# An MLP whose second stage uses eight block products in the last two visits of the first pair, and begins later in the second visit

## The chip, the cores and the metric

The kernel runs on one core of one Trainium2 chip. The metric is the device time of one execution in microseconds (us); every figure without a unit is in us. The profile comes from one execution and names the engines PE (TensorE, the matmuls), PEld (its weight loads), DVE (VectorE), ACT (ScalarE), POOL (GpSimd) and SP (SyncE, whose queue issues the DMAs).

## The reference

A transformer block on 2048 tokens of width D = 576: attention with 32 heads of 18 and one shared key and value head, then an MLP with F = 4608. The change lies in the MLP, whose core is:

```
y = layernorm(x)
h = gelu(y @ w1 + b1)        # (2048 x 576) @ (576 x 4608), tanh form
out = h @ w2 + b2            # (2048 x 4608) @ (4608 x 576)
x = x + gb * out
```

All is float32. A scale `gb` and the shift and scale ahead of `y` come from a small product of the condition vector; they are folded into the weights and into the normalised rows before the MLP starts.

## The kernel before

**Stages.** Attention takes the first 1400 us or so; while it runs, GpSimd prepares the MLP's weights and stores them in DRAM (`w1scr`, `w2scr`, `w2sum`). Then comes the MLP, a loop over 36 *visits* (`for v in range(NV)`, `NV = 2 * NG`, `NG = 18`). The tokens are taken in two *pairs* of two blocks of 512; the visits 0 to 17 serve the first pair, 18 to 35 the second. One visit does 256 of the 4608 hidden features for one pair: both stages are therefore 2 by 2 block problems (two blocks of tokens, two halves of the features or of the width).

**Precision.** A float32 number is split into a high part, rounded to the matmul's type (FP32R), and a low part, the rest. A product is three matmuls: high by high, high by low, low by high. Making a high part is a cast or a copy, making a low part a subtraction. `ops` (28 slots) and `opt` hold the parts of the first stage's inputs, `GT` (the buffers `big`, `gt` and a piece of `w1a`) those of its outputs, addressed by *unit* number.

**First stage, with seven products.** By Strassen's method, in Winograd's form, the four blocks of the first stage come from seven block products A11, S2, S3, A12, S1, A22, S4 (`product`, L1053 of the kernel before), in that order in each visit. Six matmuls of 128x512 make one; four of them take two more with the operands of width 64 that are left over (`opt`, the *tails* t0 and t1). VectorE adds the results up (`u`, L1250, L1257, L1273, L1282, L1291), and `gelu` (L1062 to L1074) runs in three steps on ScalarE and VectorE. A gelu result `h` is copied to a unit's high part by ScalarE (L1071), and GpSimd makes its low part (L1074). `psB` has four buffers in PSUM.

**Second stage, with seven products.** `sums(v)` forms four sums of the four gelu blocks on GpSimd: four additions or subtractions (L1126 to L1135), four casts (L1123) and four low parts (L1124). `fc2s(v)` then does seven *pieces*, in the order of `SEVEN`. A piece is 12 matmuls of 128x288 into two `psA` tiles of 128x576 (L1150) and two VectorE additions from them (L1156), into the output rows `XT` or into `eb`. There are two `psA` buffers. After its last use, each piece's weights are loaded anew for the next visit (`load_w2s`, one DMA of 288 KB). The very last visit (35) has no sums: `fc2` does the four blocks as eight plain block products, 96 matmuls of 128x288 in eight pieces, one `psA` tile and one addition (L1184) per 128 tokens.

**What sets the order.** The order is written by hand: each engine does its instructions in the order in which the code issues them. Between two products the loop calls `t_()` (the next piece of the second stage), `s_()` (the next sum), `g_()` (the next step of every running gelu) and `more()` (forming operands, or layernorm and output work). `fc2s(v)` is appended at the end of visit v, so its pieces run in visit v + 1; a visit has seven `t_()`, the first between A11 and S2, and the last piece of a visit's seven runs as the first of the visit after the next. Visit 1 has only six: its first piece comes between S2 and S3.

**Forming the operands of the second pair.** `op_pieces` cuts the 14 operands out of `yr`. For the second pair this is done in visits 17 and 18, each operand as soon as its slot has been used for the last time. In the code "+X" is the high part of X by ScalarE (L974), "-X" the low part (L976), "=X" a difference of two slices of `yr` (L967). The table `at` gives each operand's slot, its slice of `yr` and the engine of its low part: `ve` is VectorE, `e2` is GpSimd for the second pair. Ahead of visit 17 stand the last transposes (L152) of the layernorm, whose results ScalarE copies to `yr` (L162); the layernorm's rows lie in two buffers named `Z2`.

**DMAs.** All go through SP's queue in the order of issue. An issue that waits for a buffer holds those behind it. First-stage weights (`w1a`, eight DMAs per visit) are reloaded right after the product that used them.

Of the kernel before, what the change touches and what calls it, by code (L numbers as in the profile page):

```python
# [8 lines left out]
F32 = mybir.dt.float32  # L9
# [23 lines left out]
def block_kernel(ctx: ExitStack, tc, x, wqkv, wo, w1, b1, w2, b2, c, wmod, ident_in, out):  # L33
# [922 lines left out]
    def op_pieces(R, e2):  # L956


        at = {"B11": (0, 0, ve), "B21": (2, 2, e2), "B22": (4, 7, e2), "T2": (6, 5, ve), "T1": (8, 5, ve),
              "T3": (10, 0, ve), "T4": (12, 2, e2), "t0": (0, 4, e2), "t1": (1, 9, e2)}  # L960
        less = {"T3": (5, 0, 0), "T4": (2, 5, 2), "T1": (7, 5, 5)}
# [57 lines left out]
    EB = [px.tile([128, 4, 288], F32, name="eb"), BC[:, :2, :].rearrange("p r (h c) -> p (r h) c", c=288)]  # L1019
    W2, W2S, GT = [], [], []  # L1020

    def wo_end():
# [4 lines left out]
        a.append(W1["r"][:, 31:40].rearrange("p a b -> p (a b)").rearrange("p (f c) -> p f c", f=2))  # L1027
        W2.extend(a[:2])
        W2S.extend(t.rearrange("p f (n c) -> p (f n) c", c=288)[:, i:i + 2] for t in a for i in (0, 2))
# [6 lines left out]
    NV = 2 * NG  # L1036

    def load_w2(v):
        for l in range(2):
            sy.dma_start(W2[l].bitcast(F32), w2scr[v % NG, :, l])  # L1040

# [14 lines left out]
    def gelu(v, f, b, p):  # L1056

        u = GU["A%d%d" % (2 - b, 2 - f)][v % 2] if v == NV - 1 or (b, f) != (0, 1) else None
        h = HB[:, 2 * b + f, :]
# [25 lines left out]
    GU["A21"] = GU["S3"]  # L1085
    GU["A22"] = 6, 7

    def xb(v, b, nn, j):
# [49 lines left out]
    def fc2s(v):  # L1138

        bank = []  # L1140
        for k, (w, first, to) in enumerate(SEVEN):
            gh, gl = (unit(GU[w][v % 2], l) for l in range(2))
            for j in range(2):
# [11 lines left out]
                else:  # L1155
                    ve.tensor_tensor(o, p[:, :, :288], o, op=ALU.add)  # L1156
            if v + 2 < NV:
                load_w2s((v + 1) % NG, k)
            else:
                if k == 3:  # L1160
                    load_w2(v + 1)
                if k > 3:
                    eb_add(v, *((1, 0), (1, 1), (0, 1))[k - 4])
# [3 lines left out]
    def fc2(v):  # L1167
        h2, l2 = W2
        for bt in range(2 * NT):
            b, t = divmod(bt, NT)  # L1170
            p = psA()
            ts_ = slice(128 * t, 128 * (t + 1))
            for nn in range(2):
                cs = slice(288 * nn, 288 * (nn + 1))
                terms = []
                for f in range(2):
                    gh, gl = (unit(GU["A%d%d" % (2 - b, 2 - f)][1], l)[:, ts_] for l in range(2))
                    terms += [(gh, h2[:, f, cs]), (gh, l2[:, f, cs]), (gl, h2[:, f, cs])]
                for q, (x, y) in enumerate(terms):
                    pe.matmul(p[:, nn, :288], x, y, start=(q == 0), stop=(q == len(terms) - 1))  # L1180
            tt = 2 * NT + bt
            X = XT[:, tt, :]
            Xv = X.rearrange("p (a b) -> p a b", a=2)
            ve.tensor_tensor(Xv, p[:, :, :288], Xv, op=ALU.add)  # L1184
            sy.dma_start(out[128 * tt:128 * (tt + 1), :], X)
            yield
# [21 lines left out]
    for v in range(NV):  # L1208
# [35 lines left out]
        more("+B11", "+T4")  # L1244
        if v > 1:
            t_()
# [3 lines left out]
        ve.tensor_tensor(U[:, 0], bb, U[:, 0], op=ALU.add)  # L1250
        t_()
        g_()
# [6 lines left out]
        more("-T2 =T3", "+B22", True)  # L1259
        t_()  # L1260
        product(ba, "A12", 2, False, (0, 0))
# [15 lines left out]
        more("-T3 -B21")  # L1277
        t_()
        g_()
        product(bc, "A22", 12, False, (1, 0))  # L1280
# [5 lines left out]
        more("=T4 +t0")  # L1286
        t_()
        g_()
        product(bd, "S4", 4, False, (2, 1))
# [60 lines left out]
```

## Time and profile before

| | before |
|---|---|
| time, median of 3 runs | 2281.99 (2280.32 to 2283.00) |
| the profiled execution: its time, its span | 2280.29, 2278.5 |
| mean granted TensorE clock | 0.996 |
| MLP, first matmul of visit 1 to the end of the span | 1425.64 to 2278.5 |
| an undisturbed visit (19) | 22.84 |
| GB/s over the span | 129 (read 200.48 MB, written 93.19 MB) |
| 128x512 subtraction on POOL (L1124), x140 | 1299 ns |
| 128x512 gelu step on DVE (L1065), x144 | 684 ns |
| 128x512 ScalarE activation (L1062), x144 | 680 ns |

How to read it: busy shares are averages over stages with different limits. A row of a timeline has the start, the duration, the engine, the line, the operation, the output and inputs by name, their shapes, and in brackets the idle time of that engine just before, with the instruction that ended it. In the table of waits the columns are the waiting engine and line, what it waited for, the sum, the number of times and the longest. A stretch of the table of stretches shows the busy time of each engine with the number of instructions, then the granted TensorE clock, the DMA share and GB/s. The durations of matmuls that follow each other overlap, so their rate is read from start to start.

### The profile page before, as it was taken

The numbers are of one execution on the slowest core, as the hardware profiler recorded it, in microseconds if no ns is written. First come the engines' busy times: TensorE is split into PE (matmuls) and PEld (weight loads), VectorE is DVE, ScalarE is ACT, GpSimd is POOL, SyncE is SP. The second block draws the span as 40 slices with busy tenths as digits, with TensorE's granted clock in tenths as the row PEclk, the third lists the DMA queues.
The fourth block names the chain that finished last, engine by engine and source line by source line (L and its number), as shares of the span: only waits on it lengthen the run. The fifth ranks groups of instructions, "written<-read, shape, count | busy, mean of one in ns | idle before, by whom it ended". The sixth has DMA issues, their size and how long they took to land.

```text
span 2278.5 us, 45948 instructions
## 1 busy us (share of the span) xinstructions
PE 2241.0 (98%) x16534; PEld 1446.2 (63%) x16534; DVE 1942.0 (85%) x3435; ACT 1644.9 (72%) x3141; POOL 1506.1 (66%) x1759
## 2 busy tenths in 40 slices
PE   8999999999999999999999999999999999999999
PEld 6644545444444444444444546888888878888888
DVE  6589999999999999999999974778888777787786
ACT  5558999999999999999999997444454444343443
POOL 6503366676787787677783002888888887767676
PEclk9999999999999999999999999999999999999999
DMA  6421234433433333333331002555656557666563
GB/s 225 138 99 49 73 124 142 136 128 117 135 124 121 119 132 114 119 125 123 119 129 64 20 7 83 180 174 178 177 173 180 160 151 215 180 178 179 177 181 117
DMA packets 184229, 305.58 MB, mean 134 GB/s; under 512 B 19275, under 2 KB 77515, under 8 KB 184001
## 3 DMA queue, kind: packets, MB, share of 16 engines
q1 hardware_dynamic: 184001, 302.64, 42.1%
q8 instruction: 131, 2.15, 0.4%
q14 instruction: 97, 0.79, 0.1%
HBM read 200.48 MB, written 93.19 MB: 129 GB/s over the span
## 4 chain that ended last, share of the span: by engine, by line
PE 90%; DVE 5%; POOL 2%; ACT 2%; issue 1%; DMA 0%; ACTq 0%; POOLq 0%; DVEq 0%
PE psC L845 22%; PE psB L1053 17%; PE psA L1150 16%; PE psB L855 14%; PE psM L315 11%; PE psB L657 2%; PE psB L244 2%; DVE mx L877 2%; PE psB L865 2%; PE psB L152 1%; ACT P L857 1%; PE psA L315 1%; PE psB L199 1%; PE psA L1180 1%; PE psA L657 1%
## 5 line engine op out<-in xcount | busy, mean ns | idle before, releaser
L857 ACT ACTIVATE P<-psB 128x512 f32<-128x512 f32 x2008 | 1044.8, 619 | 45.3 <-PE psM L315 18.4
L877 DVE TENSOR_REDUCE mx<-psM 128x1 f32<-128x512 f32 x1476 | 938.1, 683 | 42.4 <-PE psB L855 19.6
L315 PE MATMUL psM<-KS,qst 64*128 64x512 f32 x1722 | 600.1, 440 | 1.1 <-DVE mx L877 0.4
L855 PE MATMUL psB<-qst,KS 64*128 64x512 f32 x2008 | 584.5, 428 | 0.6 <-DVE mx L333 0.4
L845 PE MATMUL psC<-P,V 128*32 128x256 f32 (+3 forms) x6424 | 578.8, 448 | 0.5 <-ACT O L672 0.5
L855 PEld LDWEIGHTS psB<-qst,KS 64*128 64x128 f32 x2008 | 302.2, 184 | 215.6 <-ACT P L857 132.8
L1053 PE MATMUL psB<-ops,w1a 128*128 128x512 f32 x1512 | 395.7, 397 | 0.2 <-DVE h L1068 0.2
L315 PEld LDWEIGHTS psM<-KS,qst 64*128 64x128 f32 x1722 | 274.5, 184 | 157.2 <-DVE mx L877 122.4
L1053 PEld LDWEIGHTS psB<-ops,w1a 128*128 128x128 f32 x1512 | 271.4, 189 | 45.9 <-DVE h L1068 0.4
L1156 DVE TENSOR_TENSOR XT<-psA,XT 128x576 f32<-128x576 f32 x350 | 256.4, 753 | 18.5 <-PE psA L1150 11.5
L845 PEld LDWEIGHTS psC<-P,V 128*32 128x32 f32 x6424 | 139.4, 108 | 202.9 <-issue 176.7
L1150 PE MATMUL psA<-w2s,big 128*128 128x288 f32 x1680 | 248.3, 297 | 6.4 <-POOL big L1123 2.6
L1150 PEld LDWEIGHTS psA<-w2s,big 128*128 128x128 f32 x1680 | 240.0, 190 | 21.7 <-POOL big L1123 3.5
L1124 POOL TENSOR_TENSOR big<-s,big 128x512 fp32r<-128x512 f32 x140 | 181.9, 1299 | 11.2
L1066 ACT ACTIVATE psB<-gs 128x512 f32<-128x512 f32 x144 | 86.7, 602 | 135.5 <-DVE gs L1065 135.5
L1062 ACT ACTIVATE h<-psB,b1t 128x512 f32<-128x512 f32 x144 | 98.0, 680 | 109.1 <-PE psB L1053 93.7
L875 DVE CUSTOM_DVE_ANT_0 xc<-psM,xc 128x512 f32<-128x512 f32 x246 | 166.0, 681 | 3.7 <-PE psB L855 1.2
L868 ACT ACTIVATE xc<-psB 128x512 f32<-128x512 f32 x246 | 152.9, 622 | 11.9 <-PE psM L315 11.9
L691 POOL TENSOR_TENSOR os<-O,os 128x512 fp32r<-128x512 f32 x28 | 36.1, 1290 | 150.5 <-ACT os L690 150.5
L1065 DVE SCALAR_TENSOR_TENSOR gs<-psB,h 128x512 f32<-128x512 f32 x144 | 98.5, 684 | 39.3 <-ACT psB L1063 39.3
L718 POOL TENSOR_TENSOR r<-r,r 128x256 fp32r<-128x256 f32 (+1 forms) x162 | 121.4, 749 | 13.0
L132 POOL MEMSET qst<- 32x1024 f32 x62 | 58.6, 945 | 106.8 <-PE psB L855 69.0
(198 smaller groups left out, 3238.9 us busy)
## 6 DMA issues: line engine op xcount, KB each, us to landing
w1a<-w1scr SPq DMA_DIRECT2D x252, 256.0 KB
w2s<-w2sum SPq DMA_DIRECT2D x140, 288.0 KB
w1scr<-r SPq DMA_DIRECT2D x126, 256.0 KB
w2scr<-r SPq DMA_DIRECT2D x72, 288.0 KB
w2sum<-r SPq DMA_DIRECT2D x72, 288.0 KB
w2s<-w2scr SPq DMA_DIRECT2D x70, 288.0 KB
qst<-qscr SPq DMA_DIRECT2D x192, 72.0 KB
w1a<-w2scr SPq DMA_DIRECT2D x35, 288.0 KB
```

The source lines that it names most:

```text
L315: pe.matmul(o, QST[n][64 * g:64 * g + 64, p, 128 * qt:128 * (qt + 1)], KS[64 * g:64 * g + 64, 512 * kb:512 * (kb + 1)], start=True, stop=True)
L718: po.tensor_tensor(o[:, n:2 * n], src, o[:, :n].bitcast(F32), op=ALU.subtract)
L845: pe.matmul(PVt[n][32 * j:32 * (j + 1), cs], V[:, kc, :], t[:, j, cs], start=(kc == 0 and h0 == 0), stop=(kc == 15), skip_group_check=True)
L855: pe.matmul(t, KS[64 * g:64 * g + 64, 128 * kc:128 * (kc + 1)], QST[n][64 * g:64 * g + 64, i, :], start=True, stop=True)
L857: ac.activation(P[n, kc][:, 2 * i + g, :], t, AF.Exp, scale=SCALE)
L868: ac.activation(XC[-1], t, AF.Relu)
L875: ve.tensor_tensor_reduce(c, t, c, 1.0, -3.0e38, ALU.add, ALU.max, o)
L877: ve.tensor_reduce(o, t, axis=AX.X, op=ALU.max)
L1053: pe.matmul(o, x, y, start=(first and i == 0), stop=(i == len(terms) - 1), skip_group_check=True)
L1124: po.tensor_tensor(unit(u, 1), x, unit(u, 0).bitcast(F32), op=ALU.subtract)
L1150: pe.matmul(p[:, i, :288], x[:, ts_], W2S[k][:, y], start=(bool(first) and q == 0), stop=(q == 2), skip_group_check=True)
L1156: ve.tensor_tensor(o, p[:, :, :288], o, op=ALU.add)
```

## The change

Visits 16 and 17 make no sums. Their second stage is the eight-block form that visit 35 alone had, so `fc2` now takes the visit as its argument, the dictionary `WHOLE` names the visits and the weight buffers ("a" or "b"), and `gu` gives the units: visit 17's four blocks lie in other units than visit 16's. Gelu block A21 now gets a high and a low part in these visits too. The weights are loaded in four DMAs of 288 KB: set "a" lies in the buffers of the first four pieces' weights, set "b" in the buffer of the fifth and sixth and in the two `Z2` buffers. The first seven weight loads of the second pair follow when these buffers are free. All eight pieces of visit 16 run in visit 17 (behind the last piece of visit 15), those of visit 17 in visit 18; visits 17, 18 and 19 have no `t_()` between A11 and S2. The low parts of t0 and t1 go from GpSimd to VectorE. Visit 1's first piece moves from behind S2 to behind A12, and the second and third, and the fourth and fifth, follow each other without a product between.

```diff
-              "T3": (10, 0, ve), "T4": (12, 2, e2), "t0": (0, 4, e2), "t1": (1, 9, e2)}
+              "T3": (10, 0, ve), "T4": (12, 2, e2), "t0": (0, 4, ve), "t1": (1, 9, ve)}
...
-        W2.extend(a[:2])
+        W2["a"] = [t[:, f] for t in a[:2] for f in range(2)]
+        W2["b"] = [a[2][:, f] for f in range(2)]
...
+    WHOLE = {NG - 2: "a", NG - 1: "b", NV - 1: "a"}
+
     def load_w2(v):
+        w = W2[WHOLE[v]]
+        if len(w) < 4:
+            w.extend(px.tile([128, 640], F32R, name="Z2", bufs=2)[:, :D] for _ in range(2))
         for l in range(2):
-            sy.dma_start(W2[l].bitcast(F32), w2scr[v % NG, :, l])
+            for f in range(2):
+                sy.dma_start(w[2 * l + f].bitcast(F32), w2scr[v % NG, :, l, f])
...
-        u = GU["A%d%d" % (2 - b, 2 - f)][v % 2] if v == NV - 1 or (b, f) != (0, 1) else None
+        u = gu("A%d%d" % (2 - b, 2 - f), v) if v in WHOLE or (b, f) != (0, 1) else None
...
+    def gu(w, v):
+
+        return {"A21": 1, "A11": 2, "A12": 4, "A22": 7}[w] if v == NG - 1 and v in WHOLE else GU[w][v % 2]
...
-            if v + 2 < NV:
+            if v + 1 not in WHOLE:
                 load_w2s((v + 1) % NG, k)
             else:
                 if k == 3:
                     load_w2(v + 1)
-                if k > 3:
+                elif k == 5 and v + 2 in WHOLE:
+                    load_w2(v + 2)
+                elif k == 6 and v + 2 in WHOLE:
+                    load_w2s(0, 6)
+                if v == NV - 2 and k > 3:
                     eb_add(v, *((1, 0), (1, 1), (0, 1))[k - 4])
...
-            tt = 2 * NT + bt
+            tt = 2 * NT * (v // NG) + bt
...
-            sy.dma_start(out[128 * tt:128 * (tt + 1), :], X)
+            if v == NV - 1:
+                sy.dma_start(out[128 * tt:128 * (tt + 1), :], X)
+            elif bt == 2 * NT - 1:
+                for k in range(4) if WHOLE[v] == "a" else (4, 5):
+                    load_w2s(0, k)
...
-        if v > 1:
+        if v > 1 and v - 1 not in WHOLE and v - 2 not in WHOLE:
             t_()
...
-        t_()
+        if v != 1:
+            t_()
...
-        t_()
+        if v != 1:
+            t_()
...
         t_()
+        if v == 1:
+            t_()
...
         t_()
+        if v - 1 in WHOLE:
+            t_()
+        if v == 1:
+            t_()
...
-        if v == NV - 1:
+        if v == NV - 1 or v - 1 in WHOLE:
             while f2:
                 t_()
-        if v < NV - 1:
+        if v not in WHOLE:
             sm.append(sums(v))
```

In the built kernel the lines shift: `product` is L1060, a second-stage matmul L1161 (seven products) or L1195 (eight), the low part of a gelu unit L1081, a sum's cast and low part L1134 and L1135.

GpSimd, from the forming of T1 for the second pair on (end of visit 17 and start of visit 18), before. `yr` is the source of the operands, `ops` holds their parts, `opt` those of the tails, `s` the sums, `h` the gelu results:

```order
L967 TENSOR_TENSOR yr<-yr 128x1024
L976 TENSOR_TENSOR opt<-yr,opt 128x512
L1126 TENSOR_TENSOR s<-h 128x512
L1123 CAST big<-s 128x512
L1124 TENSOR_TENSOR big<-s,big 128x512
L1129 TENSOR_TENSOR s<-h 128x512
L1130 TENSOR_TENSOR s<-s,h 128x512
L1123 CAST big<-s 128x512
L1124 TENSOR_TENSOR big<-s,big 128x512
L976 TENSOR_TENSOR ops<-yr,ops 128x1024 x2
L1074 TENSOR_TENSOR big<-h,big 128x512
L976 TENSOR_TENSOR opt<-yr,opt 128x512
```

And now, from the low part of B21 on:

```order
L976 TENSOR_TENSOR ops<-yr,ops 128x1024
L1081 TENSOR_TENSOR big<-h,big 128x512 x2
L967 TENSOR_TENSOR yr<-yr 128x1024
L976 TENSOR_TENSOR ops<-yr,ops 128x1024 x2
L1081 TENSOR_TENSOR big<-h,big 128x512
L1081 TENSOR_TENSOR gt_21023<-h,gt_21023 128x512 x2
```

Between T1 and the low parts of T4 and B22 (the row x2) nothing is left of the sums, and both tails' low parts are gone.

VectorE at the start of visit 18, from the last gelu step of visit 17 on, before (`u` is an addition of the first stage, the rows from `psA` are second-stage additions):

```order
L1068 SCALAR_TENSOR_TENSOR h<-psB,h 128x512
L976 TENSOR_TENSOR ops<-yr,ops 128x1024
L1257 TENSOR_TENSOR u<-psB,u 128x512
L1156 TENSOR_TENSOR XT<-psA,XT 128x2x288 x2
L1156 TENSOR_TENSOR eb<-psA,eb 128x576 x2
L1065 SCALAR_TENSOR_TENSOR gs<-psB,h 128x512
```

and now:

```order
L1075 SCALAR_TENSOR_TENSOR h<-psB,h 128x512
L976 TENSOR_TENSOR ops<-yr,ops 128x1024
L976 TENSOR_TENSOR opt<-yr,opt 128x512
L1277 TENSOR_TENSOR u<-psB,u 128x512
L1199 TENSOR_TENSOR XT<-psA,XT 128x576 x2
L1072 SCALAR_TENSOR_TENSOR gs<-psB,h 128x512
```

The low part of t1 stands behind that of T1, and two second-stage additions stand where four stood.

TensorE in visit 1, from A11 and S2 (the row x12) on, before:

```order
L1053 MATMUL psB<-ops,w1a 128x512 x12
L1150 MATMUL psA<-w2s,big 128x288 x12
L1053 MATMUL psB<-ops,w1a 128x512 x6
L1150 MATMUL psA<-w2s,gt_21023 128x288 x12
L1053 MATMUL psB<-ops,w1a 128x512 x6
L1053 MATMUL psB<-opt,w1a 128x512 x2
L1150 MATMUL psA<-w2s,gt_21023 128x288 x12
```

and now (A11, S2, S3 and A12 in the first two rows):

```order
L1060 MATMUL psB<-ops,w1a 128x512 x24
L1060 MATMUL psB<-opt,w1a 128x512 x2
L1161 MATMUL psA<-w2s,big 128x288 x12
L1060 MATMUL psB<-ops,w1a 128x512 x6
L1060 MATMUL psB<-opt,w1a 128x512 x2
L1161 MATMUL psA<-w2s,gt_21023 128x288 x24
```

The first piece comes two products later, and the second and third are one run of 24 matmuls.

More of the change, by code (lines that the diff above doesn't have):

```diff
@@ L1019, in block_kernel @@
     EB = [px.tile([128, 4, 288], F32, name="eb"), BC[:, :2, :].rearrange("p r (h c) -> p (r h) c", c=288)]
-    W2, W2S, GT = [], [], []
+    W2, W2S, GT = {}, [], []
     def wo_end():
@@ L1167, in fc2 @@
     def fc2(v):
-        h2, l2 = W2
+        w2 = W2[WHOLE[v]]
         for bt in range(2 * NT):
@@ L1176, in fc2 @@
                 for f in range(2):
-                    gh, gl = (unit(GU["A%d%d" % (2 - b, 2 - f)][1], l)[:, ts_] for l in range(2))
-                    terms += [(gh, h2[:, f, cs]), (gh, l2[:, f, cs]), (gl, h2[:, f, cs])]
+                    gh, gl = (unit(gu("A%d%d" % (2 - b, 2 - f), v), l)[:, ts_] for l in range(2))
+                    terms += [(gh, w2[f][:, cs]), (gh, w2[2 + f][:, cs]), (gl, w2[f][:, cs])]
                 for q, (x, y) in enumerate(terms):
                     pe.matmul(p[:, nn, :288], x, y, start=(q == 0), stop=(q == len(terms) - 1))
-            tt = 2 * NT + bt
+            tt = 2 * NT * (v // NG) + bt
             X = XT[:, tt, :]
```

## The prediction

> **What bounds the kernel now.** I read the page's busy times and chain first, then TensorE's waits over the MLP (1420 to 2278), then a table of stretches, then the timeline of the stretches that stood out.
>
> ```profile
> PE 2241.0 (98%) x16534; PEld 1446.2 (63%) x16534; DVE 1942.0 (85%) x3435; ACT 1644.9 (72%) x3141; POOL 1506.1 (66%) x1759
> PE 90%; DVE 5%; POOL 2%; ACT 2%; issue 1%; DMA 0%; ACTq 0%; POOLq 0%; DVEq 0%
> ```
>
> TensorE is the bound almost everywhere, so an added matmul costs its full time, and an edit elsewhere pays only where TensorE stands. Where does it stand in the MLP? These are its waits there:
>
> ```profile
> PE psA L1150 <- DVE XT L1156: 4.1, 2, 3.3
> PE psB L1053 <- POOL opt L976: 3.0, 1, 3.0
> ...
> PE psA L1150 <- POOL big L1123: 2.6, 2, 2.2
> ```
>
> Few and long. Cut at the first matmul of product A11, five visits (1, 2, 17, 18, 19) read:
>
> ```profile
> core 0: us, PE busy (x) PEld busy (x) DVE busy (x) ACT busy (x) POOL busy (x), PEclk, DMA share, GB/s
> 1425.64:1452.79 27.15, 24.43 (x124) 21.17 (x123) 18.28 (x29) 11.20 (x19) 21.01 (x23) 0.87 0.55 176
> 1452.79:1476.24 23.45, 23.30 (x136) 20.48 (x135) 19.95 (x34) 10.36 (x19) 21.33 (x24) 1.00 0.59 175
> 1804.98:1835.40 30.42, 25.25 (x134) 21.86 (x135) 26.06 (x31) 13.83 (x22) 29.04 (x19) 0.94 0.45 135
> 1835.40:1864.10 28.70, 25.14 (x136) 21.94 (x135) 19.94 (x30) 13.20 (x22) 25.50 (x20) 0.94 0.47 135
> 1864.10:1886.94 22.84, 22.84 (x137) 20.58 (x135) 18.13 (x27) 9.30 (x16) 16.57 (x15) 1.00 0.61 180
> ```
>
> Visit 19 is the undisturbed one: 22.84, TensorE never idle. Visits 17 and 18 together take 59.12, which is 13.44 over two such visits. Visit 1 holds one second-stage piece less (72 of its matmuls, not 84) and still takes 27.15. In 17 POOL is busy 29.04 of 30.42, and VectorE 26.06. The excess is more than idle time:
>
> ```profile
> 1430.83 0.85 PE L1150 MATMUL psA<-w2s,big 128*128 128x288 f32 x2 [2.21 <-POOL big L1123]
> 1432.17 2.77 PE L1150 MATMUL psA<-w2s,big 128*128 128x288 f32 x10 [0.50 <-POOL big L1124]
> 1434.74 2.76 PE L1053 MATMUL psB<-ops,w1a 128*128 128x512 f32 x6
> ...
> 1819.43 3.00 PE L1150 MATMUL psA<-w2s,gt 128*128 128x288 f32 x12 [3.28 <-DVE XT L1156]
> 1822.23 2.00 PE L1053 MATMUL psB<-ops,w1a 128*128 128x512 f32 x6
> 1824.53 1.73 PE L1150 MATMUL psA<-w2s,big 128*128 128x288 f32 x12
> 1826.11 1.56 PE L1053 MATMUL psB<-ops,w1a 128*128 128x512 f32 x6
> 1828.95 1.86 PE L1150 MATMUL psA<-w2s,big 128*128 128x288 f32 x12 [0.82 <-DVE XT L1156]
> 1833.74 1.82 PE L1150 MATMUL psA<-w2s,big 128*128 128x288 f32 x12 [1.07 <-issue]
> 1841.07 1.59 PE L1150 MATMUL psA<-w2s,big 128*128 128x288 f32 x10 [0.52 <-POOL big L1124]
> 1853.75 0.69 PE L1053 MATMUL psB<-opt,w1a 128*128 128x512 f32 x1 [2.98 <-POOL opt L976]
> 1854.24 3.08 PE L1150 MATMUL psA<-w2s,big 128*128 128x288 f32 x12
> ```
>
> Behind each wait of 2.2 or more the next dozen or so matmuls take up to twice as long (12 in 3.00 and 3.08, against 1.73), and the granted clock of those visits is 0.87 to 0.94. Behind 0.82 and 1.07 they do not. So a long wait removed gives back itself and about 1.7 of slow matmuls (3.00 - 1.73 plus 2.00 - 1.56). The Trainium skill (TensorE: Matmul & The Clock Gate, section What's actually happening) states that the clock halves after an idle window of about 3.4 us; the rows show the halving behind 2.98 and even 2.21 idle, so here the measurement decides.
>
> **The change part by part.** *Added matmuls.* Two visits do 96 second-stage matmuls in place of 84: 24 more. A dozen takes 1.58 from start to start (1824.53 to 1826.11), 0.132 each, so +3.16. (The 50 first-stage matmuls of a visit then have 22.84 - 84 x 0.132 = 11.8, 0.235 each; six are 1.4, eight 1.9.) Bound above by the last visit's same form, 0.138 each, +3.31:
>
> ```profile
> 2261.42 13.23 PE psA L1180 x96
> ```
>
> *Visits 17 and 18.* The eight-block form needs no sums, so each of the visits 16 and 17 sheds four additions, four casts and four low parts on POOL and gains one low part (block A21). Visit 18 is the first of the second pair, and its operands are formed in the same stretch:
>
> ```profile
> 1812.58 1.70 DVE L976 TENSOR_TENSOR ops<-yr,ops 128x1024 fp32r<-128x1024 f32 x1
> 1814.80 1.71 DVE L976 TENSOR_TENSOR ops<-yr,ops 128x1024 fp32r<-128x1024 f32 x1
> 1816.43 2.28 DVE L967 TENSOR_TENSOR yr<-yr 128x1024 f32<-128x1024 f32 x1
> 1818.64 1.41 DVE L1156 TENSOR_TENSOR XT<-psA,XT 128x576 f32<-128x576 f32 x2
> ...
> 1837.68 1.30 POOL L1126 TENSOR_TENSOR s<-h 128x512 f32<-128x512 f32 x1
> 1839.05 0.61 POOL L1123 CAST big<-s 128x512 fp32r<-128x512 f32 x1
> 1846.49 4.76 POOL L976 TENSOR_TENSOR ops<-yr,ops 128x1024 fp32r<-128x1024 f32 x2
> 1852.42 1.27 POOL L976 TENSOR_TENSOR opt<-yr,opt 128x512 fp32r<-128x512 f32 x1
> ...
> 1831.75 1.23 DVE L967 TENSOR_TENSOR yr<-yr 128x1024 f32<-128x1024 f32 x1 [0.23 <-POOL ops L976]
> ```
>
> Additions and low parts are one kind and size of operation, 1.30. Saved on POOL per visit: 4 x 1.30 + 4 x 0.61 + 4 x 1.30 - 1.30 = 11.5, so visit 17's 29.04 falls to 17.5. That ends the wait of 2.98: the low half of the second tail (-t1) stood on POOL behind one visit's sums and the 4.76 of -T4 -B22, and it now stands on VectorE, straight behind -T1. The wait of 3.28 has VectorE's forming row (1.70, 1.71, 2.28) ahead of the additions that free psA. A second-stage piece now fills one psA buffer, not two, and holds one addition. So the addition queued behind =T3 is wanted only by the third piece, after A12, a piece and S1, about 5.3 of matmuls later. Followed row by row: A11, the new wait below, S2, the old visit's last piece and S3 end on TensorE at 1811.7, and piece, A12, piece, S1 at 1818.6, where the third piece wants the first one's buffer. VectorE has -B11 from 1811.8 (1.70, POOL is busy beside it), S3's addition (0.7), then -T2 and =T3 with POOL quiet (1.23 each): 1816.6, and the addition at 1817.4. With 1.71 and 2.28, as today, it is 1818.9, 0.3 late. VectorE loses four additions of 0.75 in visit 17 and gains -t0: 26.06 becomes 23.7, in a visit of some 26.8. That is its cover; without it the old 3.28 returns.
>
> -t0 and -t1 on VectorE cost 0.69 alone and 1.93 beside POOL's work, by the rows of the same operation ahead of the MLP:
>
> ```profile
> 1407.57 0.69 DVE L976 TENSOR_TENSOR opt<-yr,opt 128x512 fp32r<-128x512 f32 x1
> 1413.15 1.93 DVE L976 TENSOR_TENSOR opt<-yr,opt 128x512 fp32r<-128x512 f32 x1
> ```
>
> I take 0.69. In visit 18 -T1 follows the first piece's addition, 5.3 into the visit, so -t1 is done by 8.0; its reader, S1, starts after four products and three pieces, 10.8 into it, so even 1.93 is hidden. The rule that speaks against the move is the Trainium skill's (SBUF — State Buffer, section SBUF: two separate sides): a VectorE operation with two SBUF inputs and a GpSimd operation hold one port pair in turn. The pair 0.69 and 1.93 agrees with it; by it the move adds at most 2 x 1.24 on VectorE, which the slack above would cover.
>
> A new wait comes at the start of 17. The piece that stood between A11 and S2 goes behind S2, and S2's bank is freed by ScalarE's copy of the last transposes:
>
> ```profile
> 1804.24 0.69 DVE L1068 SCALAR_TENSOR_TENSOR h<-psB,h 128x512 f32<-128x512 f32 x1
> 1804.27 0.69 ACT L1062 ACTIVATE h<-psB,b1t 128x512 f32<-128x512 f32 x1
> 1805.42 0.77 ACT L162 ACTIVATE yr<-psB 128x512 f32<-128x512 f32 x2
> ```
>
> Block A21's new copy (of the size of the 1804.27 row, 0.69) enters ahead of that row and waits for VectorE's h (1804.24 + 0.69), so all behind it comes 1.2 later, the copy that S2 needs near 1807.2. A11 started at 1804.98 and its six matmuls are over at 1806.4. I take 0.85, between 0 and 1.5.
>
> The weights come in four DMAs per visit (four blocks of 288 KB, not seven), issued behind the fourth piece of visit 16, more than half a visit (11.4) ahead of use; at the 135 GB/s of visit 17 these 1.18 MB take 8.7. Those bound for the Z2 buffers hold SP's queue until the transposes ahead of visit 17 have read Z2; the first-stage loads queued behind them are used a visit later. Hence nothing; without that lead TensorE would wait for them at the first new piece. The last visit's weights are the same bytes in four DMAs, not two.
>
> So visit 17 takes 22.84 + 24 x 0.132 + 0.85 = 26.85 (one piece of the old kind and all eight new ones), 18 takes 22.84 + 12 x 0.132 = 24.42, and 19, whose first piece is gone, 22.84 - 1.58 = 21.26. Sum 72.53 against 81.96: **-9.43**, the added matmuls counted.
>
> *Visit 1.* The first piece needs POOL's first sum, ready at 1432.1, and today comes behind S2, at 1428.6. Behind S3 and A12 (14 matmuls, 3.3) it starts at 1432.0, so that wait of 2.21 + 0.50 and its slow rows go. Without waits the visit takes 21.26. Its pieces now come in pairs, and a pair asks for both psA buffers twice; VectorE's additions and its gelu steps stand between:
>
> ```profile
> L1156 DVE TENSOR_TENSOR XT<-psA,XT 128x576 f32<-128x576 f32 x350 | 256.4, 753 | 18.5 <-PE psA L1150 11.5
> 1457.47 2.14 PE L1150 MATMUL psA<-w2s,big 128*128 128x288 f32 x12
> ```
>
> The second piece of a pair waits about 0.65 (a gelu step ahead of the 0.75); two pairs, 1.3, bounds 0 and a piece each, 3.16. S3 follows S2 directly and waits 0.3 for its bank. Visit 2's first piece, which took 2.14 and not 1.74, waits 0.3 longer on POOL's unmoved queue. So 21.26 + 1.6 = 22.86 and 0.3: 27.15 - 23.16 = **-3.99**.
>
> *Sum*: -13.42 on a span of 2278.5, hence 2265.1, and 2266.9 for the profiled run (2280.29); that run lies 1.70 under the median, so by the median 2281.99 - 13.42 = **2268.6**.
>
> **The rivals.** (a) *Visit 1 gains nothing*: VectorE sets its length, since all its 18.28 now falls into 22.9 and follows in pairs. Against it, 18.28 is less. 2268.6 + 4.0 = 2272.6. (b) *VectorE's forming still holds psA in 17*: 3.28, 0.82, 1.07 and 1.7 of slow matmuls stay, 6.9: 2275.5. For it, 26.06 busy; against it, one addition per piece. (c) *Only idle time returns*, the slow matmuls having another cause: idle 2.21 + 0.50 + 3.28 + 0.82 + 1.07 + 0.52 + 2.98 = 11.4, less 3.16, 0.85 and 1.9: 5.5, so 2276.5. The Trainium skill's 3.4 us window, named above, would read so, as no wait here is that long; the rows speak against it. (d) *(a) and (b) together*: 2279.5, no change that shows. (e) *Slower*: VectorE, not POOL, is late in all three visits; each keeps its length, and the matmuls and the new wait come on top: 2281.99 + 3.16 + 0.85 = 2286.0. It decides where VectorE's work in 17 passes 26.8; it is counted at 23.7.
>
> **How the numbers follow.** Forecast 0.60, (a) 0.12, (b) 0.09, (c) 0.04, (d) 0.08, (e) 0.07. A change under 0.2% (4.6) can't be told from none here, so faster 0.85, same 0.08, slower 0.07. The range reaches from all new waits at nothing (13.42 + 0.85 + 1.9 = 16.2, 2265.8) and a little below to (c): 2265.0 to 2276.5; outside lie (d) and (e).
>
> **What would show it.** Right: no wait of TensorE above 1 on POOL's opt or on VectorE's additions in visits 17 and 18, granted clock 1.00 there, POOL near 17 busy; about 26.9, 24.4 and 21.3 for visits 17 to 19; a wait under 1 ahead of 17's S2; visit 1 near 23. Wrong: VectorE named behind waits of 2 or more in 17 or 1, slow matmuls with no long wait ahead, or TensorE waiting on weights.

## The result, and the profile after

| | before | after |
|---|---|---|
| time, median of 4 runs each | 2281.15 (2280.02 to 2283.00) | 2268.34 (2267.53 to 2269.93) |
| ratio, 95% interval | | 0.9948 (0.9935 to 0.9961) |
| span of the profiled execution | 2278.5 | 2266.7 |
| first matmul of visit 1 at | 1425.64 | 1425.85 |
| from there to the end | 852.86 | 840.85 |
| visits 1, 2 | 27.15, 23.45 | 23.44, 23.25 |
| visits 17, 18, 19 | 30.42, 28.70, 22.84 | 27.93, 24.42, 21.23 |

The changed kernel is faster by 12.8 between the medians, and by 12.0 between the two traces from the first matmul of visit 1 on. The forecast was 2268.6 and a gain of 13.4. The part ahead of visit 1, which the change leaves alone, starts visit 1 at another time in each execution (1424.70 to 1428.87 in the runs below; the last section says how much of that the clock explains). So the experiments are read by the *length*, from the first matmul of visit 1 to the end of the span: it is 840.85 here and 840.97 in another profiled run of the same kernel.

The table of stretches of the changed kernel, cut at A11 as in the prediction (visits 1, 2, 17, 18, 19):

```profile
core 0: us, PE busy (x) PEld busy (x) DVE busy (x) ACT busy (x) POOL busy (x), PEclk, DMA share, GB/s
1425.85:1449.29 23.44, 22.32 (x123) 18.89 (x122) 18.84 (x31) 11.99 (x20) 21.25 (x23) 1.00 0.67 203
1449.29:1472.54 23.25, 23.08 (x137) 20.59 (x136) 19.21 (x32) 9.57 (x18) 21.13 (x24) 1.00 0.65 177
1801.31:1829.24 27.93, 26.76 (x159) 23.73 (x159) 23.94 (x30) 17.37 (x28) 14.70 (x9) 1.00 0.40 126
1829.24:1853.66 24.42, 24.42 (x148) 22.14 (x147) 17.96 (x23) 12.20 (x20) 13.46 (x8) 1.00 0.45 133
1853.66:1874.89 21.23, 21.23 (x125) 18.97 (x123) 15.36 (x23) 7.90 (x14) 15.02 (x14) 1.00 0.64 179
```

The granted clock is 1.00 in all five. GpSimd fell from 29.04 to 14.70 in visit 17 (by 14.3, where 11.5 was forecast) and from 25.50 to 13.46 in visit 18, and TensorE is busy in all of visits 18 and 19. What TensorE still waits for in the MLP, the largest rows that name an engine (sum, times, longest):

```profile
PE psA L1161 <- DVE XT L1167: 1.2, 3, 0.5
PE psA L1161 <- POOL big L1135: 1.0, 2, 0.8
PE psB L1060 <- ACT yr L162: 0.6, 1, 0.6
PE psA L1195 <- DVE XT L1199: 0.5, 1, 0.5
```

Before, single waits of 3.3, 3.0 and 2.2 stood here; now none of these passes 0.8. Where the remaining ones lie in visits 1, 17 and 20, from TensorE's timeline:

```profile
1438.36 1.88 PE L1161 MATMUL psA<-w2s,gt 128*128 128x288 f32 x12 [0.42 <-DVE XT L1167]
...
1444.16 1.85 PE L1161 MATMUL psA<-w2s,big 128*128 128x288 f32 x12 [0.46 <-DVE XT L1167]
...
1803.62 1.66 PE L1060 MATMUL psB<-ops,w1a 128*128 128x512 f32 x6 [0.63 <-ACT yr L162]
...
1824.25 0.66 PE L1195 MATMUL psA<-w2s,big 128*128 128x288 f32 x3 [0.54 <-DVE XT L1199]
...
1876.81 1.82 PE L1161 MATMUL psA<-w1a,big 128*128 128x288 f32 x12 [0.36 <-DVE XT L1167]
```

The first two are the second pieces of visit 1's pairs, the third is S2 of visit 17. The last two the prediction does not have. The one of 0.36 is new: it stands at the first piece of visit 20, which takes 23.40 in place of 23.06, and why VectorE's addition comes late there was not followed. The two waits on a sum's parts (L1135) lie in visits 2 and 21. What VectorE and GpSimd did around the wait of 0.54:

```profile
1811.78 1.21 DVE L967 TENSOR_TENSOR yr<-yr 128x1024 f32<-128x1024 f32 x1
1812.92 1.41 DVE L1199 TENSOR_TENSOR XT<-psA,XT 128x576 f32<-128x576 f32 x2
...
1821.22 2.31 DVE L967 TENSOR_TENSOR yr<-yr 128x1024 f32<-128x1024 f32 x1 [0.81 <-POOL ops L976]
1823.45 1.41 DVE L1199 TENSOR_TENSOR XT<-psA,XT 128x576 f32<-128x576 f32 x2
...
1837.34 1.78 DVE L976 TENSOR_TENSOR opt<-yr,opt 128x512 fp32r<-128x512 f32 x1
```

```profile
1817.28 1.55 POOL L1081 TENSOR_TENSOR w1a<-h,gt 128x512 fp32r<-128x512 f32 x1 [6.51 <-ACT gt L1078]
1818.80 2.39 POOL L976 TENSOR_TENSOR ops<-yr,ops 128x1024 fp32r<-128x1024 f32 x1
```

The rows at 1811.78 and 1812.92 are =T3 and the addition behind it, which the prediction walked through: the addition frees its psA buffer 1.4 before the third piece starts at 1815.05. The row at 1821.22 is =T4. It waits 0.81 for GpSimd's -B21 (1818.80), which stood behind a low part of gelu that GpSimd itself had waited 6.51 for. =T4 then takes 2.31 beside GpSimd's next operation, and the addition behind it comes at 1823.45, 0.54 too late for a piece. The last row is -t1, in visit 18.

### The profile page after: what moved, and what is told of

It reads as the page before. It is cut to its first block, busy times and chain, and to the rows that moved or that the text cites. A ratio compares the mean times of both kernels' runs of the same rounds, so it can differ in the third digit from the quotient of the medians.

```text
span 2266.7 us, 45924 instructions
## 1 busy us (share of the span) xinstructions
PE 2235.6 (99%) x16558; PEld 1445.1 (64%) x16558; DVE 1936.4 (85%) x3425; ACT 1645.3 (73%) x3143; POOL 1478.3 (65%) x1735
## 4 chain that ended last, share of the span: by engine, by line
PE 90%; DVE 4%; POOL 2%; ACT 2%; DMA 1%; issue 1%; SPq 0%; ACTq 0%; POOLq 0%
PE psC L845 22%; PE psB L1060 17%; PE psA L1161 15%; PE psB L855 14%; PE psM L315 11%; PE psB L657 3%; PE psB L244 2%; DVE mx L877 2%; PE psB L865 2%; PE psA L1195 2%; PE psB L152 1%; ACT P L857 1%; PE psA L315 1%; PE psB L199 1%; PE psA L657 1%
## 5 line engine op out<-in xcount | busy, mean ns | idle before, releaser
L857 ACT ACTIVATE P<-psB 128x512 f32<-128x512 f32 x2008 | 1044.5, 619 | 45.2 <-PE psM L315 19.3
L1060 PE MATMUL psB<-ops,w1a 128*128 128x512 f32 x1512 | 393.9, 396 | 1.0 <-ACT yr L162 0.6
L1060 PEld LDWEIGHTS psB<-ops,w1a 128*128 128x128 f32 x1512 | 270.4, 188 | 47.4 <-ACT yr L162 1.1
L1167 DVE TENSOR_TENSOR XT<-psA,XT 128x576 f32<-128x576 f32 x330 | 241.7, 753 | 14.4 <-PE psA L1161 7.8
L1161 PEld LDWEIGHTS psA<-w2s,big 128*128 128x128 f32 x1584 | 224.0, 188 | 14.7 <-POOL big L1135 1.5
L1161 PE MATMUL psA<-w2s,big 128*128 128x288 f32 x1584 | 230.8, 295 | 1.7 <-POOL big L1135 1.0
L1135 POOL TENSOR_TENSOR big<-s,big 128x512 fp32r<-128x512 f32 x132 | 170.7, 1293 | 10.6
L1078 ACT ACTIVATE big<-h 128x512 fp32r<-128x512 f32 x39 | 24.7, 633 | 146.2 <-DVE h L1075 146.2
```

The costliest lines, as they stand in the source:

```text
L857: ac.activation(P[n, kc][:, 2 * i + g, :], t, AF.Exp, scale=SCALE)
L1060: pe.matmul(o, x, y, start=(first and i == 0), stop=(i == len(terms) - 1), skip_group_check=True)
L1135: po.tensor_tensor(unit(u, 1), x, unit(u, 0).bitcast(F32), op=ALU.subtract)
L1161: pe.matmul(p[:, i, :288], x[:, ts_], W2S[k][:, y], start=(bool(first) and q == 0), stop=(q == 2), skip_group_check=True)
```

## The experiments

**Each part by itself.** Four kernels: visit 1's part alone, the tails' low parts alone, and the changed kernel without each of them.

`v1_only`, the kernel before with this edit (its first part stands twice, behind S2 and behind S3):

```diff
-        t_()
+        if v != 1:
+            t_()
...
         more("-T3 -B21")
         t_()
+        if v == 1:
+            t_()
...
         more("=T4 +t0")
         t_()
+        if v == 1:
+            t_()
```

> The kernel before with visit 1's pieces moved, nothing else. Theory (a long wait costs itself and the slow matmuls behind it): visit 1 goes from 27.15 to about 23.4 and visit 2 from 23.45 to 23.25 as in the changed kernel, so the span falls by 3.9, from 2278.5 to 2274.6; visits 17 and 18 keep 30.42 and 28.70. Rival (only idle time returns, the slow matmuls come from something else): 2.71 of waits go, 1.1 of new ones come, so the span falls by 1.6 to 2276.9 and visit 1 keeps a granted clock below 0.95.

Measured: visit 1, and then four stretches of 3.41 from the attention far ahead of it:

```profile
1428.87:1451.98 23.11, 22.03 (x123) 18.93 (x122) 18.93 (x31) 12.00 (x20) 20.90 (x23) 1.00 0.64 206
...
132.70:136.12 3.42, 2.25 (x9) 0.86 (x8) 3.05 (x5) 0.27 (x1) 1.21 (x1) 1.00 0.37 121
136.12:139.53 3.41, 3.32 (x13) 2.44 (x13) 2.76 (x4) 0.00 (x0) 0.00 (x0) 0.50 0.32 97
139.53:142.95 3.42, 3.42 (x13) 2.32 (x13) 2.33 (x4) 2.68 (x6) 0.00 (x0) 0.50 0.68 195
142.95:146.36 3.41, 3.41 (x14) 1.59 (x16) 3.15 (x6) 3.40 (x7) 0.00 (x0) 0.50 1.03 395
```

The span is 2277.8, and by itself that reads as a gain of 0.7. But visit 1 began at 1428.87, 3.23 later than in the kernel before, in code that is the same: here three stretches in a row ran at half clock, in the trace of before only one (its row stands in the last section). That explains a part: from ScalarE's row of L355 (132.10 before, 133.14 here) to its row of seven L857 (146.90 and 149.32) it takes 14.80 before and 16.18 here, so 1.4 is lost there; 1.0 was lost ahead of it, and the rest comes behind it at full clock, from a cause that stays open. By the length, 2277.8 - 1428.87 = 848.93, visit 1's part is worth 852.86 - 848.93 = 3.93, and all of it lies in visits 1 and 2 (23.11 and 23.56, together 46.67 for 50.60). So the theory's 3.9 holds, the rival's 1.6 is out, and the clock is 1.00. The times alone would not settle it: the ratio is 0.9994 (0.9984 to 1.0003), which holds the rival's 1.6 (0.9993) and ends just short of 3.93 (0.9983). Whether this kernel's other executions also began visit 1 late stays open, since only one was profiled.

`tails_only`, the kernel before with one line changed:

```diff
-"t0": (0, 4, e2), "t1": (1, 9, e2)}
+"t0": (0, 4, ve), "t1": (1, 9, ve)}
```

> The kernel before with the low parts of t0 and t1 on VectorE, nothing else. Theory of the prediction (the wait of 2.98 in visit 18 is GpSimd's queue ahead of -t1): the wait goes with its 1.35 of slow matmuls, so visit 18 falls from 28.70 to about 24.4 and the span by 4.3 to 2274.2; visit 17 keeps 30.4. Rival (VectorE is late as well, or the sums behind GpSimd's queue end the next wait): 1.9 more on VectorE or a wait on the sums' parts takes over, visit 18 stays above 27 and the span falls by less than 1.5.

Measured, visits 1, 17 and 18:

```profile
1426.12:1452.45 26.33, 23.30 (x123) 20.34 (x122) 18.28 (x29) 11.20 (x19) 21.00 (x23) 0.94 0.57 185
...
1804.68:1835.33 30.65, 26.22 (x135) 22.87 (x135) 25.03 (x31) 13.87 (x22) 28.40 (x19) 0.89 0.47 135
1835.33:1860.32 24.99, 23.54 (x136) 20.38 (x135) 22.16 (x32) 13.20 (x22) 23.85 (x18) 1.00 0.54 154
```

Visit 18 fell by 3.71, to 24.99, and the wait of 2.98 is gone, so GpSimd's queue ahead of -t1 was its cause. Two smaller waits of TensorE, 0.81 on VectorE's additions and 0.58 on a gelu unit's low part, took a part of it back, and so the 4.3 is 3.71. Visits 17 and 18 together fell by 3.48. The length, 2275.1 - 1426.12 = 848.98, is 3.88 less than before, but that is not all the edit's: visit 1, which the edit leaves alone, took 26.33 and not 27.15, since one stretch at half clock followed its long wait and not two. The ratio is 0.9995 (0.9985 to 1.0004); 3.48 would be 0.9985, the end of that interval.

`tails_pool` is the changed kernel with that line undone (`ve` back to `e2`).

> The changed kernel with the low parts of t0 and t1 back on GpSimd. Theory (the freed sums alone empty GpSimd's queue, and -t1 would end there near 1840, its reader starts at 1841.5): the span stays within 0.5 of 2266.7 and visit 18 at 24.4. Rival, as the prediction has it (moving -t1 to VectorE is needed): a wait on opt of 1.5 to 3 returns in visit 18, and the span rises to 2268 to 2271.

Measured, the end of -t1 on GpSimd, and S1's tail matmuls on TensorE:

```profile
1840.41 1.29 POOL L976 TENSOR_TENSOR opt<-yr,opt 128x512 fp32r<-128x512 f32 x1
```

```profile
1842.51 0.63 PE L1060 MATMUL psB<-opt,w1a 128*128 128x512 f32 x2
```

-t1 ends at 1841.7, 0.8 ahead of its reader, and nothing waits. Visits 17 and 18 take 27.93 and 24.43, the length is 2267.7 - 1426.88 = 840.82, that of the changed kernel. So moving the tails is worth about 3.5 by itself and nothing beside the freed sums: both end the same wait, and either would have done. The ratio is 0.9958 (0.9944 to 0.9972).

`no_v1` is the changed kernel with the conditions on visit 1 taken out (pieces again behind S2 and S3, no pairs).

> The changed kernel without visit 1's part. Theory (the parts don't touch each other): visit 1 takes 27.15 again and visit 2 23.45, the span is 3.9 over 2266.7, so 2270.6; visits 17, 18 and 19 keep 27.9, 24.4 and 21.2. Rival (a slow visit 1 is caught up later, for a queue behind it is what sets the end): the span rises by less than 2.

Measured, visit 1:

```profile
1426.26:1453.41 27.15, 24.43 (x123) 21.15 (x122) 18.26 (x29) 11.18 (x19) 20.96 (x23) 0.87 0.56 176
```

Visit 1 is back at 27.15, visits 17 to 19 are unchanged (27.93, 24.43, 21.22); the length is 2271.0 - 1426.26 = 844.74, 3.89 over the changed kernel. The parts add up: 3.9 from visit 1, 8.1 from the rest. The ratio to before is 0.9970 (0.9961 to 0.9979); the median lies 3.0 over that of `tails_pool`, which ran beside it.

**The excess of visit 17.** It ran 1.1 over the prediction's sum. `old_piece_back` edits the changed kernel at the two waits:

```diff
-        if v > 1 and v - 1 not in WHOLE and v - 2 not in WHOLE:
+        if v == NG - 1 or v > 1 and v - 1 not in WHOLE and v - 2 not in WHOLE:
             t_()
...
-        more("+T3 +B21", "-B22", True)
+        more("+T3 +B21 -B21", "-B22", True)
...
-        more("-T3 -B21")
+        more("-T3")
```

> The changed kernel with two edits in visit 17: the last piece of visit 15 stands between A11 and S2 again, and the low part of B21 is issued to GpSimd directly behind its high part. Theory (the 1.1 by which visit 17 ran over its sum lies in two waits, 0.63 on ScalarE's copy ahead of S2 and 0.54 on VectorE's additions, which stood behind =T4, which stood behind -B21 on GpSimd): both go, visit 17 falls from 27.93 to 26.0 to 26.2 (22.84 and two dozen matmuls at 0.132), and first matmul of visit 1 to the end falls from 840.85 to 839.1. Rival (VectorE's forming is what is late, whatever the order): =T4 still ends a wait of 0.5 or more on psA in visit 17, which stays above 27.

Measured, visit 17, and =T4 on VectorE:

```profile
1803.88:1830.03 26.15, 26.15 (x159) 23.87 (x160) 23.37 (x30) 16.04 (x27) 14.33 (x8) 1.00 0.43 134
```

```profile
1824.34 1.22 DVE L967 TENSOR_TENSOR yr<-yr 128x1024 f32<-128x1024 f32 x1
```

TensorE is busy for all of visit 17. It takes 26.15, which is 22.84 and 24 matmuls at 0.138; =T4 waits for nothing and takes 1.22. The length is 2267.5 - 1428.55 = 838.95, 1.9 under the changed kernel's. The ratio to before is 0.9941 (0.9927 to 0.9954).

**GpSimd's eb additions.** Visit 21 has waits of 0.28 and 0.81 on a sum's parts (0.36 and 0.81 in the kernel before). `eb_early` adds to `old_piece_back` that GpSimd's first two additions of eb rows run in visit 18:

```diff
+                if v == NG and half in ("=T4 +t0", "=T1 +T4 -t0 +B22 +t1"):
+                    step(fill)
...
-        if v == NG + 1:
+        if v == NG:
             fill.append(pair_end())
```

> As old_piece_back, and GpSimd's additions of the eb rows for the first pair begin at the end of visit 18, where GpSimd is busy only 13.5 of 24.4, in place of visit 20. Theory (the waits of 0.28 and 0.81 on a sum's parts in visit 21 come from these additions, 8.4 in a row with the sums): they go, another 1.2 of length, to 837.9 from the first matmul of visit 1. Rival (GpSimd's queue is late in every visit and only moves its wait): a wait of 0.8 or more on a sum's parts in visit 19 or 20, and nothing gained.

Measured, on GpSimd and at the first piece of visit 19:

```profile
1846.35 5.60 POOL L1109 TENSOR_TENSOR XT<-XT,eb 128x576 f32<-128x576 f32 x4
```

```profile
1855.27 1.58 PE L1161 MATMUL psA<-w2s,big 128*128 128x288 f32 x10 [0.82 <-POOL big L1135]
```

The rival was right. Both additions (two instructions each) stood in a row ahead of the visit's first sum, which began at 1851.90, and the same two waits (0.27 and 0.82) moved from visit 21 to visit 19. The length is 2263.6 - 1424.70 = 838.90, nothing gained; the ratio is 0.9943 (0.9930 to 0.9955). `eb_spread` therefore steps `pair_end` only behind A22 (`half == "=T4 +t0"`) in visits 18, 19 and 20, where GpSimd stands waiting for gelu results.

> As old_piece_back, and the three additions of eb rows go one by one to visits 18, 19 and 20, each behind A22, where the sums of the visit are over and GpSimd waits for gelu results. Theory (eb_early only moved the wait because its second addition stood ahead of visit 18's sums): no wait on a sum's parts is left in visits 19 to 22, and the length from the first matmul of visit 1 falls from 838.95 to 837.8; against the changed kernel 840.85 that is 3.1, a ratio to it of 0.9986. Rival (GpSimd has no room of 2.8 in any of these visits without being late for the next first piece): a wait of 0.3 or more on a sum's parts in visits 19 to 21, and the length stays within 0.5 of 838.95.

Measured: no wait on a sum's parts behind visit 2, the length is 2264.6 - 1426.68 = 837.92. The ratio is 0.9936 (0.9922 to 0.9949). The changed kernel ran beside it:

> The changed kernel as it is, beside the next kernel on one chip. First matmul of visit 1 to the end 840.85 within 0.1, as before; the time 0.994 to 0.996 of the kernel before, the spread coming from ahead of visit 1.

Its length is 2266.6 - 1425.63 = 840.97, its ratio 0.9952 (0.9939 to 0.9964).

**What sets visits 1 and 2.** `pairs_first` is `eb_early` with the first piece of each pair of visit 1 issued ahead of the gelu step:

```diff
         ve.tensor_tensor(be, bd, U[:, 1], op=ALU.add)
+        if v == 1:
+            t_()
         g_()
...
         t_()
-        if v == 1:
-            t_()
```

and in the same way behind A22.

> As eb_early, and in visit 1 the first piece of each pair is issued ahead of the gelu step, so that VectorE does its additions ahead of the 0.69 step. Theory (the waits of 0.42 and 0.46 at the pairs' second pieces are this step): both go, visit 1 falls from 23.44 to 22.6, the length to 837.1. Rival (the later gelu step delays GpSimd's parts, which visit 1 is as short of): the waits on a sum's parts in visit 2 grow by 0.5 or more and nothing is gained.

Measured, visits 1 and 2, and a wait of TensorE in visit 2:

```profile
1426.64:1448.96 22.32, 22.03 (x123) 18.94 (x122) 18.81 (x30) 11.82 (x20) 20.11 (x23) 1.00 0.68 216
1448.96:1473.35 24.39, 23.36 (x137) 20.52 (x135) 19.42 (x33) 9.65 (x18) 22.24 (x24) 1.00 0.59 169
```

```profile
1455.10 1.59 PE L1161 MATMUL psA<-w2s,big 128*128 128x288 f32 x10 [0.81 <-POOL big L1135]
```

Both pair waits went and visit 1 fell to 22.32, but visit 2 rose by 1.1: together 46.71, against 46.69 in the changed kernel and 46.67 in `v1_only`. The length is 2265.7 - 1426.64 = 839.06, nothing gained, the ratio 0.9943 (0.9930 to 0.9955). The rival named the sign, but not the reason: GpSimd's parts came no later. The row above starts 28.46 behind visit 1's A11, and the same matmuls start 28.44 to 28.48 behind it in the changed kernel (both profiled runs), in `v1_only` and in `eb_spread`. GpSimd's queue in the changed kernel, from the end of visit 1, says what sets that moment (no row has idle time in brackets):

```profile
1448.01 1.44 POOL L617 TENSOR_TENSOR Z<-Z,BC 128x576 f32<-128x576 f32 x1
1449.52 1.43 POOL L618 TENSOR_TENSOR Z<-Z,BC 128x576 f32<-128x576 f32 x1
1450.90 1.30 POOL L1137 TENSOR_TENSOR s<-h 128x512 f32<-128x512 f32 x1
```

GpSimd works without a gap from visit 0's sums to visit 1's first, and two layernorm operations (L617, L618) stand ahead of that sum, which visit 2's first piece needs. `norm_later` joins `eb_spread` and the pairs of `pairs_first`, and holds the layernorm steps back in the second half of visit 1:

```diff
-            elif 0 < v < NG and fill and (room or mark[0] != "T"):
+            elif 0 < v < NG and fill and (v > 1 or half[:1] != "=") and (room or mark[0] != "T"):
```

> As eb_spread, with visit 1's pairs as in pairs_first, and with the layernorm step that stood on GpSimd ahead of visit 1's first sum (two operations of 1.43) behind that visit's second sum. Theory (visits 1 and 2 together are set by GpSimd's queue, which has no gap from visit 0's last sum to visit 1's first; so 46.7 for both visits whatever the order of the pieces): the waits of 0.22 and 0.81 on a sum's parts in visit 2 go, visits 1 and 2 take 22.56 and 22.9, 45.4 in place of 46.7, and the length from the first matmul of visit 1 falls from 837.92 to 836.6. Rival (TensorE and VectorE set these visits): visit 1 falls to 22.56, and visit 2 stays above 24 or another wait takes the place.

Measured, visits 1 and 2:

```profile
1426.41:1448.80 22.39, 22.09 (x124) 19.00 (x123) 18.88 (x30) 11.86 (x20) 20.04 (x22) 1.00 0.68 212
1448.80:1471.82 23.02, 23.02 (x136) 20.44 (x135) 19.40 (x33) 8.85 (x16) 21.38 (x23) 1.00 0.63 183
```

Together 45.41, the length 2262.8 - 1426.41 = 836.39. This is the shortest length of all, 4.5 under the changed kernel's. The time is 2264.59 (2263.62 to 2266.80), a ratio to before of 0.9934 (0.9920 to 0.9947), which by itself can't be told from that of `eb_spread`.

**What a wait costs beyond itself.** `waits_put_in` is the changed kernel with additions whose results nothing uses:

```diff
         bb = psB()
+        for _ in range(1 + v % 3 if 3 <= v <= 15 else 0):
+            ve.tensor_tensor(bb, U[:, 0], U[:, 0], op=ALU.add)
         product(bb, "S2", 6)
```

> The changed kernel with one, two or three idle additions of VectorE (128x512, about 0.69 each) ahead of S2 in visits 3 to 15, on whose result S2 waits: waits of about 1.6, 2.3 and 3.0, so 13 waits. It tells what a wait costs beyond itself. Theory A (the clock is granted in stretches of 3.41 us on a fixed grid, and a stretch in which TensorE was busy less than some 1.5 to 2 is followed by one at half clock): every slow stretch lasts 3.41 or a multiple, costs 1.7 of matmuls, and follows a stretch with little work; waits of 1.6 cause none, those of 3.0 all do, those of 2.3 some, by where they fall on the grid. Theory B (idle must last 3.4 at a stretch): none of the 13 is followed by slow matmuls, granted clock 1.00 throughout. Theory C (each wait of 2.2 or more is followed by slow matmuls at once): all waits of 2.3 and 3.0 are, at once.

The waits came out longer than planned, 1.46 to 5.35, since other work stood between the additions on VectorE. Four of the 13, on TensorE:

```profile
1480.37 1.67 PE L1060 MATMUL psB<-ops,w1a 128*128 128x512 f32 x6 [1.46 <-DVE psB L1268]
1508.71 2.10 PE L1060 MATMUL psB<-ops,w1a 128*128 128x512 f32 x6 [4.33 <-issue]
1538.33 2.92 PE L1060 MATMUL psB<-ops,w1a 128*128 128x512 f32 x6 [4.79 <-DVE psB L1268]
1567.39 2.71 PE L1060 MATMUL psB<-ops,w1a 128*128 128x512 f32 x6 [2.62 <-DVE psB L1268]
```

The three waits of 1.46 left the matmuls at speed (6 in 1.67); with all ten of 2.62 and more came half-clock stretches. Theory B (3.4 of idle at a stretch) is out: 2.62 was enough, as 2.21 was in the kernel before. Theory C is out too: behind 4.33 the six matmuls took 2.10 and not 2.9, because the slow stretch began only at the next line of a grid. The same run cut on that grid (busy time of TensorE second, granted clock third from the end):

```profile
1478.93:1482.34 3.41, 1.98 (x10) 1.71 (x11) 1.63 (x3) 0.00 (x0) 3.33 (x3) 1.00 0.34 89
...
1506.23:1509.65 3.42, 0.94 (x4) 0.84 (x5) 2.34 (x2) 0.00 (x0) 3.20 (x4) 1.00 0.20 69
1509.65:1513.06 3.41, 3.41 (x14) 3.13 (x14) 1.45 (x2) 0.00 (x0) 1.84 (x4) 0.50 0.26 77
...
1533.54:1536.95 3.41, 0.01 (x1) 0.00 (x0) 3.31 (x5) 0.00 (x0) 3.33 (x3) 1.00 0.41 109
1536.95:1540.37 3.42, 2.04 (x5) 1.65 (x6) 1.33 (x1) 0.00 (x0) 3.00 (x3) 0.50 0.00 0
1540.37:1543.78 3.41, 3.41 (x15) 3.22 (x14) 1.45 (x2) 0.00 (x0) 0.00 (x0) 0.50 0.27 77
```

The stretch with 1.98 of work was followed by full clock, one with 0.94 or 0.01 by half clock, and a half-clock stretch with 2.04 of work by another. Theory A stands, with its bound a little under the 1.5 to 2 that it gave: a stretch with 1.55 of work at full clock (from 1502.82) was followed by full clock. Waits near 2.3, which were to go either way, did not occur.

## Why the prediction was right

*Added matmuls* (+3.16). Visit 18, where TensorE is never idle, takes 24.42: 22.84 and twelve matmuls at 0.132, to the digit. Visit 19, a piece shorter, takes 21.23 (21.26 was forecast).

*Slow matmuls behind long waits* (1.7 each). Right in size. 1.7 is one stretch of 3.41 at half clock, and visit 1 had two in a row, which the sum held too, since it took that visit's length from its matmuls. Rival (c), that only idle time returns, fell with `v1_only`. The prediction weighed it with the Trainium skill (TensorE: Matmul & The Clock Gate, section What's actually happening), read as 3.4 of idle at a stretch. The Trainium skill (same section) also says that the window is free-running, 3413 ns long, and that its place differs from run to run; with that the traces agree, whose stretches last 3.41.

*The wait of 2.98.* Gone, as forecast, but for one reason more than was needed. The prediction named two, the freed sums and -t1 on VectorE; `tails_only` and `tails_pool` show that either ends it, and that the second is worth nothing beside the first. On VectorE -t1 took 1.78 beside GpSimd, within the 1.93 that was allowed for. GpSimd's load in visit 17 came to 14.70, not 17.5, because the prediction counted every row of the sums at 1.30 or 0.61: three of those in visit 17 of before (1813.15, 1815.51 and 1817.69) took 2.28, 2.12 and 1.49 while VectorE formed operands, and all twelve 15.5. That error only left more slack.

*The wait of 3.28.* Gone by the walk that was made for it. =T3 ended 11.7 after A11's start (11.6 in the walk), and psA came free 1.4 ahead of need (1.2). Two sizes in the walk were wrong and made up for each other: -B11 took 1.41 (1.70 in the walk), -T2 1.71 (1.23). No run separates the shorter =T3 (1.21, where before had 2.28) from the later need for the buffer; by the prediction's own count the old sizes would have been 0.3 late.

*The new wait ahead of S2* (0.85). 0.63 idle, and 2.31 from A11's start to S2's where six matmuls take 1.40: 0.91 lost. The mechanism and the size were right.

*Visit 17* (26.85 forecast, 27.93 measured). This is the term that was mis-sized, and the step is VectorE's walk, which ended at =T3. It counted VectorE's load (23.7 forecast, 23.94 measured) and took a visit of 26.8 as cover for all that followed. =T4 waits for -B21 on GpSimd, and the row of before showed that wait too (0.23). GpSimd had been relieved, but by its order -B21 still stood behind a gelu low part that comes when ScalarE has made the high part. It cost 0.54 idle and 0.4 in restarting. `old_piece_back` removed both waits by order alone, with the same work on every engine, and visit 17 came to 26.15.

*Visit 1* (22.86 forecast, 23.44 measured; with visit 2, -3.99 forecast, -3.91 measured). The two pairs cost 0.63 each from start to start (0.65 forecast), S3's bank 0.35 (0.3); most of the rest is 0.4 around A12's tail, which the sum had not and which is of that execution: in the other profiled run of the same kernel visit 1 took 23.12 and visit 2 23.61, so that only their sum, 46.7, is steady. What was missed is what these waits rest on: `pairs_first` took the pair waits away and visit 2 gave all of it back. GpSimd's queue sets the two visits, so the pair waits cost nothing, and visit 2's 0.3 on that queue, in the forecast an afterthought, is what decided; what they would cost with the shorter queue of `norm_later` was not run. Rival (a), VectorE as what sets visit 1's length, fell, and so did (b), (d) and (e), which need VectorE late in visit 17 by 3 where it was late by 0.54.

*Weights and DMAs.* No wait of TensorE on a load in visits 17 to 19, as forecast.

*The sum.* -12.01 in the traces from visit 1 on, against -13.42: 1.1 of the difference is visit 17, and 0.34 is visit 20, where the sum had nothing. That the predicted time came within 0.3 of the median owes something to chance: one more run of the kernel before (2280.02), taken beside the change, lowered that kernel's median by 0.84 against the one that the forecast started from.

## What to carry to other kernels

When one engine's load is cut, the waits on it end only where its *order* lets them: walk each later operation that another engine waits for to its place in the queue, and don't let a busy share stand for that. Before shortening a wait, ask whether the visit's length is set by it: here two orders of the same pieces gave 46.7 for two visits, and only moving other work of GpSimd's queue behind its sums made them shorter than that. Compare executions from a point where they have the same past; here the start of the stage under test moved by 4 between executions, which is as much as visit 1's part of the change was worth.

## What the runs showed of the hardware

The granted clock changes on a fixed grid of 3.41 and is 1.00 or 0.50. The kernel before, cut on its grid, once in the attention and then around the wait of visit 1; behind the last row the clock is 1.00 again:

```profile
140.40:143.82 3.42, 3.42 (x14) 1.65 (x18) 3.40 (x6) 3.39 (x8) 0.00 (x0) 0.50 0.98 368
...
1427.23:1430.64 3.41, 1.38 (x6) 0.76 (x5) 2.80 (x6) 2.96 (x5) 2.72 (x3) 1.00 1.04 372
1430.64:1434.06 3.42, 2.73 (x10) 2.39 (x11) 1.37 (x4) 0.00 (x0) 3.26 (x4) 0.50 0.15 54
1434.06:1437.47 3.41, 3.41 (x11) 2.84 (x11) 1.59 (x3) 0.00 (x0) 3.19 (x5) 0.50 0.29 89
```

In the traces of before, of the change, of `v1_only`, `tails_only` and `waits_put_in` all stretches of the MLP fit one rule: busy time times granted clock of 1.38 or less in a stretch (2.73 at 0.50 is 1.37) is followed by half clock, 1.49 or more (2.98 at 0.50 in `waits_put_in`, from 1594.98) by full clock. The Trainium skill (TensorE: Matmul & The Clock Gate, section What's actually happening) has this window, free-running and 3413 ns long; the stretches of 3.41 agree. So a wait of 2.2 to 3.3 in a stage that TensorE bounds was followed by one or two stretches at half clock, each worth up to 1.7, by where it fell on the grid: behind the same wait of 2.21 in visit 1 there were two in the trace of before and one in that of `tails_only`. In the attention the rule is another: there 2.25 of work at full clock was followed by half clock, and three full stretches at half clock followed each other. Three of the thirteen profiled executions (`v1_only`, `old_piece_back`, `waits_put_in`) had three such stretches in a row there, and in them visit 1 began latest, at 1428.4 to 1428.9; in the other ten it began between 1424.70 and 1426.88. The spread among those ten the clock does not explain: the second profiled run of the changed kernel had no stretch at half clock ahead of visit 1 and began it at 1425.63, `eb_early` had one and began it at 1424.70.
